# Batch 0's v on ScalarE's queue, chunks ahead of x, in the space of the later MLP weights

## The chip, the cores and the metric

One core of a Trainium2 chip runs the kernel. The metric is the device time of one execution in microseconds, the median of the timed runs; before the change this is 1745.4 us (three runs, 1744.48 to 1746.48). The core has TensorE (PE, products into PSUM), VectorE (DVE), ScalarE (ACT) and GpSimd (POOL), and SyncE (SP), which here only issues transfers. Transfers between HBM and SBUF run on 16 DMA engines; SyncE and ScalarE each have a queue from which they issue them. An engine works through its instructions in order; an instruction that waits holds up all behind it on that engine, transfers to be issued included.

## The reference

```python
def _attn_ref(x, v, pos_emb, w1, w2):            # x, v: [2, 12480, 128]
    h_mlp = np.maximum(pos_emb @ w1, 0.0) @ w2   # pos_emb [12480, 64]
    h_filt = h_mlp * np.exp(-0.01 * pos)[:, None]
    u = x * v
    Uf = np.fft.rfft(u, n=2 * S, axis=1); Hf = np.fft.rfft(h_filt, n=2 * S, axis=0)
    y = np.fft.irfft(Uf * Hf[None], n=2 * S, axis=1)[:, :S]
    return x * y
def _moe_ref(x, w_in, w_out):                    # 24960 tokens, 128 -> 2048 -> 128
    h = x @ w_in
    return np.maximum(0.01 * h, h) @ w_out
```

The output is the second function of the first: a long convolution of u = x * v with a filter from a small MLP over the positions, times x, then an MLP with 2048 hidden units. The weights `w_in` and `w_out` arrive as float64.

## The kernel before, in words

The convolution is a transform in two steps over token numbers n = 128 a + b (a up to 98, b up to 128), with spectra kept in HBM between the steps. For batch 0 the kernel has three stages: the first transforms along a (products with the constant `cf`, tiles `ft` and `f1`), the second along b, with the filter's product and the way back, and the third, the long one, transforms back and runs the MLP. Batch 1's convolution is a generator (`conv1`) whose pieces are taken in between. The instruction order is written out by hand (`manual_schedule`): every engine and every queue runs what the program text gives it, in that order.

The change lies in the first stage (from line 181, to about 166 us in the trace, its last store to 173). It has 16 chunks (`NC0 = HB // MC`) of 4 token columns for both halves p, each tile on 98 partitions:

- `load_pos(q)` fetches the positions of four chunks, `load_a(c)` fetches `ft`, x and v of a chunk (and `f1` for the first two). `load_tokens` issues three transfers for one tensor: 96 partitions, one partition, and the short last row (lines 68 and 70). In `load_a` all are on SyncE's queue; `ft` has 5 buffers, x and v 3 each.
- `prep(c)` multiplies x by v into `uh` (L212, on GpSimd, for chunk 0 on VectorE), computes `f1` from `ft` for chunks past the second (L221, L235, L236), and applies the small MLP to the positions (transposes L229, copy L232 on ScalarE, product L240, L243).
- For each of a chunk's four columns TensorE writes a PSUM tile `a` of three buffers (L315), and `add_sub` evacuates it: ScalarE copies one half to `a1s` (L99), VectorE forms sum and difference into the chunk's result `o` (L101, L103). `o` has two buffers.
- The result goes to HBM (`scr1`) in two transfers (L288). The store of chunk c-1 is kept in `late` and issued at the top of chunk c, behind `load_a(c + 3)`. So SyncE's order at the top of a chunk is: loads for three chunks on, positions if due, the store of the chunk before.
- `prep(c + 2)` is run in three steps between the columns of chunk c.
- At chunk 2 SyncE issues six small constant loads (`mb`, `mi`, `mi2`, L268 to L272), at chunk 7 `w22`, and at chunk 13 the first loads of batch 1 (`fetch_a(0)`). In the last chunk, one-row copies (`direct`, L308) and an early load (`early`, L303) bring `bin0`, the first tile of the second stage; the last store follows the last copies. The second stage's loads `bin` (L514) and the raw weights (L526, L527) stand behind it on SyncE's queue.
- The MLP weights live in four tiles of 8 KB per partition (`w_in_h`, `w_in_l`, `w_out_h`, `w_out_l`), taken from the pool `const` at the start (lines 52 to 55) and written only in the second stage (`weights`, L541 to L556).

## Time and profile before

| what | value |
|---|---|
| timed runs, median (lowest to highest) | 1745.4 us (1744.48 to 1746.48) |
| profiled execution, span from first to last instruction | 1742.2 us |
| busy share of the span: PE, DVE, ACT, POOL | 96%, 61%, 56%, 33% |
| transfers on SyncE's queue, on ScalarE's | 223.71 MB, 25.69 MB |
| mean rate of all transfers | 144 GB/s |

The profiled execution's own time is known by its span, 1742.2 us; the timed median has 3.2 us more, which lie around the first and last instruction or between two executions. The shares are means over the whole span, in which the third stage has most of the time; the first stage has 10% of it and other limits. A row of a view is read with its columns: in a table by stretch, the busy time of each engine in it, TensorE's granted clock as a share of full speed, the share of their time in which the 16 DMA engines were busy, and the rate at which they moved bytes.

### The profile page before, as it was taken

Reading aid. Unit: us, or ns where it says so; the run is one execution under the profiler, and the core shown is the slowest. Engines: PE = TensorE matmul, PEld = TensorE weight load, DVE = VectorE, ACT = ScalarE, POOL = GpSimd, SP = SyncE. Lnnn points to the kernel's source line nnn. Section 1 sums busy time; section 2 is a strip of 40 time slices with the busy share of each in tenths; the row PEclk is TensorE's granted clock in tenths of the full one; section 3 lists DMA queues with packets and bytes.
Section 4 is the critical chain, followed back from the end, with each engine's and each line's share of the span. In section 5 each row is a group of like instructions: output and inputs, shape, how many; then the busy total and the mean of one; then the engine's idle time right before and its main releaser. Section 6 shows DMA issues by size and latency. Waiting matters only on the chain.

```text
span 1742.2 us, 26075 instructions
## 1 busy us (share of the span) xinstructions
PE 1679.3 (96%) x9159; PEld 1383.3 (79%) x9159; DVE 1060.0 (61%) x1687; ACT 973.7 (56%) x1875; POOL 579.3 (33%) x474
## 2 busy tenths in 40 slices
PE   6788899899999999999999999999999999999998
PEld 6677555598888888888888888888888888888888
DVE  4566688744544555565555554567666676667665
ACT  1222455344444466666666665666666666666666
POOL 3453122232232165565555662222112121212110
PEclk9889899989999999999999999999999999999999
DMA  9998999865666565656555642312112121212110
GB/s 231 253 274 250 310 337 325 276 177 164 188 178 177 145 168 147 173 160 162 155 155 144 184 130 71 88 53 66 57 52 73 42 66 52 64 44 73 52 31 19
DMA packets 147687, 251.07 MB, mean 144 GB/s; under 512 B 10835, under 2 KB 96930, under 8 KB 144484
## 3 DMA queue, kind: packets, MB, share of 16 engines
q1 hardware_dynamic: 127412, 223.71, 45.9%
q10 hardware_dynamic: 20144, 25.69, 4.2%
q8 instruction: 73, 1.20, 0.3%
q14 instruction: 58, 0.48, 0.1%
HBM read 165.86 MB, written 83.43 MB: 143 GB/s over the span
## 4 chain that ended last, share of the span: by engine, by line
PE 81%; DMA 10%; DVE 5%; issue 1%; SPq 1%; ACT 1%; POOL 1%; ACTq 0%; DVEq 0%; POOLq 0%
PE mh L735 10%; PE acc L768 10%; PE mh L737 10%; PE acc L767 10%; PE acc L769 10%; PE mh L736 10%; PE yp L719 7%; PE cv L132 4%; PE cv L353 3%; DMA xt<-in_x_dram 2%; DMA ft<-in_cf_dram 2%; PE op L791 2%; DMA scr<-o 1%; DMA hspec<-hs 1%; PE xp L711 1%
## 5 line engine op out<-in xcount | busy, mean ns | idle before, releaser
L742 DVE SCALAR_TENSOR_TENSOR rl<-mh,rh 128x512 fp32r<-128x512 f32 (+2 forms) x400 | 269.1, 677 | 304.3 <-ACT rh L741 299.5
L752 DVE TENSOR_TENSOR rl<-r,rh 128x512 fp32r<-128x512 f32 (+1 forms) x400 | 292.5, 744 | 148.2 <-ACT rh L751 141.3
L735 PE MATMUL mh<-zh,w_in_h 128*128 128x512 f32 (+3 forms) x800 | 328.4, 411 | 2.8 <-DVE rl L742 1.5
L741 ACT ACTIVATE rh<-mh 128x512 fp32r<-128x512 f32 (+2 forms) x400 | 235.3, 591 | 157.0 <-PE mh L737 148.1
L768 PE MATMUL acc<-rl,w_out_h 128*128 128x512 f32 (+3 forms) x800 | 310.9, 389 | 0.1
L737 PE MATMUL mh<-zh,w_in_l 128*128 128x512 f32 (+3 forms) x800 | 310.4, 388 | 0.0
L767 PE MATMUL acc<-rh,w_out_h 128*128 128x512 f32 (+3 forms) x800 | 310.3, 388 | 0.0
L769 PE MATMUL acc<-rh,w_out_l 128*128 128x512 f32 (+3 forms) x800 | 310.0, 387 | 0.0
L736 PE MATMUL mh<-zl,w_in_h 128*128 128x512 f32 (+3 forms) x800 | 309.6, 387 | 0.0
L747 ACT ACTIVATE r<-mh 128x512 f32<-128x512 f32 (+1 forms) x400 | 235.7, 590 | 129.0 <-PE mh L737 115.1
L728 POOL TENSOR_TENSOR zl<-zf,zh 128x390 fp32r<-128x390 f32 (+24 forms) x110 | 67.9, 631 | 660.8 <-ACT zh L727 514.3
L768 PEld LDWEIGHTS acc<-rl,w_out_h 128*128 128x128 f32 x800 | 150.4, 188 | 38.5 <-DVE rl L752 8.3
L737 PEld LDWEIGHTS mh<-zh,w_in_l 128*128 128x128 f32 x800 | 150.8, 188 | 31.9
L769 PEld LDWEIGHTS acc<-rh,w_out_l 128*128 128x128 f32 x800 | 150.4, 188 | 30.3
L767 PEld LDWEIGHTS acc<-rh,w_out_h 128*128 128x128 f32 x800 | 150.4, 188 | 30.2
L735 PEld LDWEIGHTS mh<-zh,w_in_h 128*128 128x128 f32 x800 | 151.2, 189 | 27.7 <-DVE rl L742 4.1
L736 PEld LDWEIGHTS mh<-zl,w_in_h 128*128 128x128 f32 x800 | 151.4, 189 | 23.5 <-DVE zl L728 0.3
L749 DVE CAST rh<-r 128x512 fp32r<-128x512 f32 (+1 forms) x200 | 115.6, 578 | 31.2 <-ACT r L747 28.4
L719 PEld LDWEIGHTS yp<-g,cp 98*128 98x128 f32 x1024 | 125.7, 194 | 5.5 <-issue 0.5
L751 ACT CAST rh<-r 128x512 fp32r<-128x512 f32 (+1 forms) x200 | 122.3, 612 | 6.3
L719 PE MATMUL yp<-g,cp 98*128 98x97 f32 (+1 forms) x1024 | 125.0, 276 | 0.2 <-issue 0.2
L727 ACT CAST zh<-zf 128x390 fp32r<-128x390 f32 (+24 forms) x111 | 37.7, 380 | 154.0 <-DVE zf L722 154.0
(133 smaller groups left out, 2328.1 us busy)
## 6 DMA issues: line engine op xcount, KB each, us to landing
cin<-scr SPq DMA_DIRECT2D x64, 392.0 KB
hd<-hspec SPq DMA_DIRECT2D x48, 512.0 KB
g<-in_cg_dram SPq DMA_DIRECT2D x65, 300.1 KB
scr<-o SPq DMA_DIRECT2D x32, 588.0 KB
bin<-scr SPq DMA_DIRECT2D x23, 768.0 KB
scr1b<-o SPq DMA_DIRECT2D x32, 392.0 KB
xm<-in_x_dram SPq DMA_DIRECT2D x65, 192.0 KB
hspec<-hs ACTq DMA_DIRECT2D x48, 256.0 KB
```

Of the source, the lines that this page charges most:

```text
L719: nc.tensor.matmul(yp[:, at:at + n], ci_t[:, r, m, p, :], g[:, r, p, m, :n], start=(r == 0), stop=(r == 1))
L735: nc.tensor.matmul(hp, w_in_h[:, fs], zh, start=True, stop=False)
L736: nc.tensor.matmul(hp, w_in_h[:, fs], zl, start=False, stop=False)
L737: nc.tensor.matmul(hp, w_in_l[:, fs], zh, start=False, stop=True)
L741: nc.scalar.activation(out=rh, in_=hp, func=AF.Relu)
L742: nc.vector.scalar_tensor_tensor(out=rl, in0=hp, scalar=0.0, in1=rh, op0=ALU.max, op1=ALU.subtract)
L747: nc.scalar.activation(out=r, in_=hp, func=AF.Lrelu, alpha=0.01)
L751: nc.scalar.copy(rh, r)
L752: nc.vector.tensor_tensor(out=rl, in0=r, in1=rh, op=ALU.subtract)
L767: nc.tensor.matmul(ap, w_out_h[:, f, :], rh, start=(f == 0 and at0[k] >= S), stop=False)
L768: nc.tensor.matmul(ap, w_out_h[:, f, :], rl, start=False, stop=False)
L769: nc.tensor.matmul(ap, w_out_l[:, f, :], rh, start=False, stop=(f == NF - 1))
```

## The change

v of batch 0 no longer comes with x in `load_a`. A new function `load_v(upto)` issues v's loads on ScalarE's queue, chunk by chunk, up to a given number of chunks. They go into halves of four tiles of a new pool `wp`; the four tiles of the MLP weights take the same space (`tag` w0 to w3) after the first stage. `load_v(1)` stands ahead of all other loads, `load_v(3)` behind `load_a(1)`, and at the top of chunk c stands `load_v(min(2 * c + 5, c + 8))`, ahead of `load_a(c + 3)`. x has four buffers in place of three, `o` three in place of two.

```diff
--- before.py
+++ after.py
@@ -49,10 +49,7 @@
 
     ident = const.tile([128, 128], F32, name="ident")
     mb = const.tile([128, 2, 2, 64], F32, name="mb")
-    w_in_h = const.tile([128, DFF], F32R, name="w_in_h")
-    w_in_l = const.tile([128, DFF], F32R, name="w_in_l")
-    w_out_h = const.tile([128, NF, D], F32R, name="w_out_h")
-    w_out_l = const.tile([128, NF, D], F32R, name="w_out_l")
+    wp = ctx.enter_context(tc.tile_pool(name="wp", bufs=1, reuse_waits="tile"))
     wc_h = const.tile([128, D], F32R, name="wc_h")
     wc_l = const.tile([128, D], F32R, name="wc_l")
     mb_h = const.tile([128, 2, 128], F32R, name="mb_h")
@@ -61,13 +58,13 @@
     mi_h = const.tile([128, 2, 128], F32R, name="mi_h")
     mi_l = const.tile([128, 2, 128], F32R, name="mi_l")
 
-    def load_tokens(t, src, m0, n):
+    def load_tokens(t, src, m0, n, q=nc.sync):
 
         full = src[: ROWS * NB, :].rearrange("(a p n) d -> a p n d", p=2, n=HB)
         for r in (slice(0, R0), slice(R0, ROWS)):
-            nc.sync.dma_start(out=t[r], in_=full[r, :, m0:m0 + n, :])
+            q.dma_start(out=t[r], in_=full[r, :, m0:m0 + n, :])
         last = src[ROWS * NB + m0:ROWS * NB + m0 + n, :]
-        nc.sync.dma_start(out=t[ROWS:], in_=last[None, None, :, :].to_broadcast([1, 2, n, last.shape[1]]))
+        q.dma_start(out=t[ROWS:], in_=last[None, None, :, :].to_broadcast([1, 2, n, last.shape[1]]))
 
     def from_float64(pool, dst, src, n):
 
@@ -185,7 +182,19 @@
             w1bd = sba.tile([128, 128], F32, name="w1bd", bufs=1)
             mi = s0.tile([128, 2, 128], F32, tag="mi", name="mi", bufs=1)
             PQ = 16
-            pos_t, f_t, xv_t, uh_t, f1_t = {}, {}, {}, {}, {}
+            pos_t, f_t, x_t, uh_t, f1_t = {}, {}, {}, {}, {}
+            vbuf = []
+            for w in range(4):
+                t = wp.tile([128, DFF], F32, tag=f"w{w}", name="vt")
+                for i in range(2):
+                    vbuf.append(t[:NA, i * 1024:i * 1024 + 1024].rearrange("a (p m d) -> a p m d", p=2, d=D))
+            v_t = []
+
+            def load_v(upto):
+                while len(v_t) < min(upto, HB // MC):
+                    t = vbuf[len(v_t) % len(vbuf)]
+                    load_tokens(t, v[0], len(v_t) * MC, MC, nc.scalar)
+                    v_t.append(t)
             rot = sba.tile([NA, 2, NA], F32, name="rot", bufs=1)
 
             def load_pos(q):
@@ -195,18 +204,16 @@
             def load_a(c):
                 ft = sba.tile([NA, MC, 2 * NA], F32, tag="ft", name="ft", bufs=5)
                 nc.sync.dma_start(out=ft, in_=cf[:, c * MC:(c + 1) * MC, 0])
-                xt = sba.tile([NA, 2, MC, D], F32, tag="xt", name="xt", bufs=3)
-                vt = sba.tile([NA, 2, MC, D], F32, tag="vt", name="vt", bufs=3)
+                xt = sba.tile([NA, 2, MC, D], F32, tag="xt", name="xt", bufs=4)
                 load_tokens(xt, x[0], c * MC, MC)
-                load_tokens(vt, v[0], c * MC, MC)
-                f_t[c], xv_t[c] = ft, (xt, vt)
+                f_t[c], x_t[c] = ft, xt
                 if c < 2:
                     f1_t[c] = sba.tile([NA, MC, 2 * NA], F32, tag="f1", name="f1", bufs=3)
                     nc.sync.dma_start(out=f1_t[c], in_=cf[:, c * MC:(c + 1) * MC, 1])
 
             def prep(c):
 
-                xt, vt = xv_t.pop(c)
+                xt, vt = x_t.pop(c), v_t[c]
                 uh = sba.tile([NA, 2, MC, C0], F32, tag="uh", name="uh", bufs=3)
                 uh_t[c] = uh
                 (nc.gpsimd if c else nc.vector).tensor_tensor(out=uh[:, :, :, FO:], in0=xt, in1=vt, op=ALU.mult)
@@ -246,6 +253,8 @@
 
             NC0 = HB // MC
             DIR, EARLY = 1, 1
+            AHEAD_V = 8
+            load_v(1)
             load_pos(0)
             nc.vector.memset(w1bd, 0.0)
             for i in range(2):
@@ -255,11 +264,13 @@
             nc.sync.dma_start(out=win, in_=cw)
             nc.sync.dma_start(out=rot, in_=cr)
             load_a(1)
+            load_v(3)
             run(prep(0))
             load_a(2)
             run(prep(1))
             late = []
             for c in range(NC0):
+                load_v(min(2 * c + 5, c + AHEAD_V))
                 if c + 3 < NC0:
                     load_a(c + 3)
                     if (c + 3) * MC % PQ == 0:
@@ -280,7 +291,7 @@
                 late = []
                 uh, ft, f1 = uh_t.pop(c), f_t.pop(c), f1_t.pop(c)
                 nxt = prep(c + 2) if c + 2 < NC0 else iter(())
-                o = sba.tile([NA, 2, MC, 2, C0], F32, tag="o", name="o")
+                o = sba.tile([NA, 2, MC, 2, C0], F32, tag="o", name="o", bufs=3)
 
                 def store(m0, n, o, c=c):
                     for ri in range(2):
@@ -327,6 +338,10 @@
                     late.append(lambda store=store, o=o: store(0, MC, o))
 
 
+        w_in_h = wp.tile([128, DFF], F32R, tag="w0", name="w_in_h")
+        w_in_l = wp.tile([128, DFF], F32R, tag="w1", name="w_in_l")
+        w_out_h = wp.tile([128, NF, D], F32R, tag="w2", name="w_out_h")
+        w_out_l = wp.tile([128, NF, D], F32R, tag="w3", name="w_out_l")
         sc = ctx.enter_context(tc.tile_pool(name="sc", bufs=2, reuse_waits="tile"))
         psc = {}
         N1 = HB // MC1
```

## Rows read from the trace of the kernel before

**Rows 1.** The page's slices: DMA busy share in tenths, 40 equal slices.

```profile
DMA  9998999865666565656555642312112121212110
```

**Rows 2.** Waits, first stage: who waited for whom, us, times, longest.

```profile
DVE o L101 <- DMA scr<-o: 42.0, 12, 7.1
...
SPq L288 <- DMA ft<-in_cf_dram: 9.7, 9, 2.6
```

**Rows 3.** Busy times by stretch: us, engines' busy us (count), PEclk, DMA share, GB/s.

```profile
8.00:12.00 4.00, 2.85 (x14) 2.43 (x13) 0.00 (x0) 0.97 (x2) 0.00 (x0) 1.00 0.72 172
12.00:44.00 32.00, 25.78 (x134) 24.16 (x135) 17.77 (x29) 6.07 (x13) 16.68 (x10) 0.89 0.99 253
44.00:52.00 8.00, 6.39 (x44) 6.05 (x42) 3.76 (x8) 2.31 (x5) 4.95 (x3) 1.00 0.61 166
...
83.50:91.40 7.90, 7.90 (x54) 7.88 (x53) 5.81 (x11) 2.68 (x6) 3.96 (x3) 0.93 0.99 297
...
108.70:120.50 11.80, 7.76 (x29) 6.48 (x30) 5.81 (x11) 1.93 (x4) 4.89 (x3) 0.63 0.92 245
...
144.60:150.30 5.70, 4.58 (x27) 3.81 (x25) 5.70 (x11) 1.44 (x3) 1.88 (x2) 1.00 0.89 267
```

**Rows 4.** Transfers issued from 0 to 170 us: queue, count, size of one.

```profile
scr<-o SPq DMA_DIRECT2D x32, 588.0 KB
xt<-in_x_dram SPq DMA_DIRECT2D x16, 384.0 KB
...
ft<-in_cf_dram SPq DMA_DIRECT2D x16, 300.1 KB
pos<-in_pos_emb_dram SPq DMA_DIRECT2D x4, 768.0 KB
```

**Rows 5.** The chain that ended last: start us, us, what.

```profile
0.73 6.33 DMA pos<-in_pos_emb_dram
```

**Rows 6.** SyncE's issues in order of time: start us, us, line, transfer.

```profile
7.08 0.59 SPq L70 DMA_DIRECT2D xt<-in_x_dram  x1
7.71 1.23 SPq L68 DMA_DIRECT2D vt<-in_v_dram  x2
...
45.02 2.45 SPq L272 DMA_DIRECT2D mi<-in_ci_dram  x4
```

**Rows 7.** TensorE in order of time within one chunk.

```profile
87.32 0.81 PE L315 MATMUL a<-uh,ft 98*98 98x192 f32 x4
...
87.97 0.81 PE L315 MATMUL a<-uh,f 97*98 97x192 f32 x4
...
88.63 0.50 PE L229 MATMUL pt<-ident,pos 98*128 98x98 f32 x4
...
90.27 1.04 PE L240 MATMUL hp<-w1bd,pts 128*98 128x128 f32 x8
```

**Rows 8.** ScalarE's queue in the second stage: two issues each.

```profile
173.03 1.22 ACTq L650 DMA_DIRECT2D hspec<-hs  x2
...
183.92 2.29 ACTq L650 DMA_DIRECT2D hspec<-hs  x2
```

**Rows 9.** Busy times by stretch around the second stage, columns as in rows 3.

```profile
176.00:180.00 4.00, 1.95 (x16) 1.60 (x16) 0.42 (x1) 0.00 (x0) 0.00 (x0) 0.59 1.01 357
154.00:160.00 6.00, 3.29 (x21) 2.97 (x19) 1.87 (x4) 0.96 (x2) 2.35 (x1) 0.97 0.92 336
180.00:260.00 80.00, 76.98 (x621) 44.24 (x622) 63.74 (x139) 38.87 (x78) 15.31 (x12) 0.96 0.99 325
```

**Rows 10.** VectorE and SyncE at the end of the first stage, by time.

```profile
159.13 0.56 DVE L101 TENSOR_TENSOR o<-a,a1s 98x384 f32<-98x384 f32 x1 [4.13 <-DMA scr<-o]
...
160.18 2.57 SPq L308 DMA_DIRECT2D bin<-o  x4
...
162.85 0.85 SPq L303 DMA_DIRECT2D bin<-scr  x2
...
166.30 0.96 SPq L288 DMA_DIRECT2D scr<-o  x2
```

## The prediction

> **What bounds the kernel now.** The change touches the first 173 of 1742 us, so I read the page's slices first: the DMA row stands at 9, 9, 9, 8 in the first four of forty slices of 43.6 us [rows 1]. Next the list of waits in the first stage: VectorE stands 42.0 us, twelve times, before its addition into `o` (L101), each time until an earlier store of `o` has landed [rows 2]. That looks as if a third `o` would bring up to 42 us. The third view, busy times by stretch, says why it doesn't: in the same stretches the 16 DMA engines are 0.92 to 0.99 busy [rows 3]. VectorE waits for a store because that store stands in a full line of transfers; take this wait away, and the next one is for the loads in the same line. One chunk moves two stores of 588 KB, x and v of 384 KB each and 300 KB of `ft` [rows 4], 2.30 MB; at the 297 GB/s of 83.5 to 91.4 us that takes 7.7 us, and this stretch, one chunk without positions, lasts 7.9 [rows 3]. The engines could go faster: VectorE is busy 5.81 us of those 7.9 [rows 3], and TensorE's pairs of products come 0.65 us apart when nothing holds them, so eight pairs with 0.50 and 1.04 us of the next chunk's preparation make 6.7 us [rows 7]. So transfers bound the stage, the engines lie 1 us per chunk behind them, and what counts is (a) the time in which the DMA engines stand idle, (b) the rate at which they move bytes, (c) how the last chunk reaches the second stage. The change takes no byte away.
>
> **The sum's base.** The span of the profiled execution is 1742.2 us, 3.2 us under the 1745.4 us median of the timed runs; I take differences within the span and put them on the median.
>
> **What the change moves.** Of nine transfers that SyncE issues per chunk, three (v) go to ScalarE's queue, into the two halves of four 8 KB tiles that later hold the MLP weights. There are eight halves, so a half comes round after eight chunks, when its product is long done: no wait there, and the weights are written only in the second stage. x gets a fourth buffer and `o` a third. The order of v against x changes: v of chunk 0 first of all, chunks 1 and 2 before `prep(0)`, then two chunks of v per chunk of work until it is some five ahead.
>
> **(1) Gaps that are there now.** Against the 0.99 of 12 to 44 us, the DMA engines miss 0.27 x 4.0 = 1.1 us at 8 to 12 us, and 0.38 x 8.0 = 3.0 us at 44 to 52 us, where SyncE issues six small constant loads one behind the other (four of them take 2.45 us of issue) [rows 3, 6]. Later they miss 0.07 x 11.8 = 0.8 at 108.7 us and 0.10 x 5.7 = 0.6 at 144.6 [rows 3]. That is 4.1 us early and 1.4 us late. Late, when all v is loaded, a chunk has six transfers in place of nine, so that more of the next can be under way: I take -1.4 us there (ends -1.4 and 0), and the early ones within (2).
>
> **(2) Gaps that are new.** The compiled program gives its transfers eight completion semaphores in turn, in program order over both queues, so an issue waits until the transfer eight places before it has landed, whoever issued it. The trace shows it: the ninth issue (x, L70) starts at 7.08 us, when the first (positions) has landed at 0.73 + 6.33 = 7.06 [rows 5, 6]; and SyncE's store issues stand 9.7 us, nine times, for loads of `ft` that a store has no use for [rows 2]. With the change this ties the queues together. ScalarE's v issues stand at the top of a chunk; behind them wait its copies `a1s` (L99), then VectorE's `o` and TensorE's PSUM buffers. The third v issue of a chunk waits for `ft` of the chunk before; at chunk 2 one waits for the positions, at chunk 3 one for the small constants. In turn SyncE's x issue of the first chunks waits until a v has landed that ScalarE can issue only when it gets there. An issue takes 0.6 us (two of v on SyncE 1.23 [rows 6]; on ScalarE's queue two take 1.22, or 2.29 where the second had to wait [rows 8]): 1.8 us per chunk of v, 3.7 in chunks 0 to 3, and meanwhile TensorE can run ahead into three PSUM buffers.
>
> I laid the first 67 us out issue by issue with the trace's own times. The positions' 0.79 MB at 253 GB/s take 3.1 of their 6.33 us [rows 3 to 5], so 3.2 us go by between an issue and its first byte and between last byte and landing. At the same rate an x or v takes 1.6 us and an `ft` 1.2, and a chunk's stores 3.6 at 336 GB/s [rows 9]. `ft` of chunk 0 then waits for v's landing (6.8 us), chunk 0's first copy comes at 27 us, and gaps of 1 to 3 us open each time both queues hang on a landing: about 8, 24, 32, 40, 52, 57 and 66 us, 10.6 us together. At the same unhindered rates the kernel before moves, until 67 us, seven x, v and `ft`, two `f1`, two positions, three and a half chunks of stores and 1.6 us of constants: 53.6 us of 64.7, 11.1 us of gaps. So the two come out even, by then five chunks of v are in, and a chunk and a half of stores is behind. I take +1.0 us, with the 4.1 us of (1) inside. Ends: -4 (the old gaps filled, none new) and +6.5 (10.6 against the 4.1 that rows 3 show).
>
> **(3) The rate.** With v on a second queue, loads and stores run side by side more often. No second queue works in the first stage; the nearest rows are from the second, where both do: 357 GB/s at 176 to 180 us and 325 at 180 to 260, against 336 for stores nearly alone on one queue [rows 9] and 253 where loads predominate [rows 3]. Sixteen v of 1.3 us (at 297 GB/s), each beside another transfer, are some 42 us with both queues in use. At 325/0.99 in place of 297/0.99 GB/s they shrink by 8.5%, 3.6 us: I take -3.6, since those are the nearest rows with two queues, though their tiles are of all 128 partitions. Ends: 0, and -6.1 if each v goes from 253 to 336 GB/s (16 x 0.38). I take no loss: in no row are two queues slower than one.
>
> The Trainium skill speaks against this term: "DMA: Bandwidth & Descriptors", section "Issuing engines are not separate DMA queues", says that transfers begun by several engines run on the same 16 DMA engines and interleave, so that a second issuer saves only issue time. By that the gain would be 3.6 us smaller.
>
> **(4) The tail.** VectorE's first `o` of the last chunk waits 4.13 us, until 159.13, for the store of two chunks before. SyncE then issues four one-row copies into `bin0` from 160.18, the early load of `bin0` at 162.85, four more copies, and the last store at 166.30 [rows 10]; the second stage's first full load waits for that store. With a third `o` the results are 4 us earlier, the first copies go while the two stores before are still moving, and the early load goes when these land. That saves at least the 0.3 us in which the later copies wait, at most this and the 2.57 us of the first copies: ends -0.3 and -2.9. I take -1.0, because the line of stores is full until about the first copies. All that follows moves along, since the second stage starts with transfers again (0.99 busy from 180 to 260 us [rows 9]).
>
> **(5) At nothing.** SyncE's saved issues (covered by the transfers under way; without that cover 1.8 us per chunk), the fourth x (x waits for no buffer now), and other places in SBUF.
>
> **Sum:** +1.0 - 1.4 - 3.6 - 1.0 = -5.0 us, 1745.4 - 5.0 = **1740.4 us**.
>
> **The rivals.**
> *A, one pool of engines, no rate gained:* (3) is 0, and +1.0 - 1.4 - 1.0 leaves 1744.0 us. For it: shares near 1 already [rows 3], so that only gaps can be won.
> The skill's rule above would end here too.
> *B, the queues chain each other (slower):* ScalarE's issues at the tops of chunks 0 to 3 come late, SyncE's loads hang on them, and the DMA engines run dry: +6.5 for (2), 0 for the late gaps and (3), -1.0 for the tail: 1750.9 us. For it: store issues that already stand for foreign loads [rows 2], the ninth issue [rows 5, 6], and a computing engine now in the same chain. Against it: the gaps are short, and the engines have 1 us of room per chunk. It decides when the DMA engines miss more than some 9 us between 12 and 68 us. That v doesn't get ahead as the change says belongs here: its third issue hangs on `ft` of one chunk before.
> *C, full overlap:* (3) at -6.1, (2) at -1: -9.5, 1735.9 us. Against it: TensorE bounds a chunk at 6.7 us.
>
> **How the numbers follow.** Forecast 0.40, A 0.27, B 0.21, C 0.12. A measurement of this kernel tells about 0.2% (3.5 us) from no change, so faster means under 1741.9: forecast and C, 0.52; same 0.27; slower 0.21. The range takes in the forecast, A, C with the long end of the tail, and the nearer half of B: 1733.5 to 1748.5. Forecast and C alone have 1733.5 to 1742.
>
> **What would show it.** (1): no stretch of 8 us with a share near 0.6 around 44 us. (2): idle in front of `a1s` at the tops of chunks 0 to 3, released by loads; the first `a1s` near 27 us. (3): over 297 GB/s in chunks 4 to 8. (4): no wait for a store before the last `o`, and the last store before 166 us. VectorE's 42 us of waits for stores should be near nothing. I am wrong if the last store goes out later although the rate rose (then the gaps of (2) are larger), or over 8 us earlier (then transfers did not bound as I say, and the `o` wait was a cause of its own).

## The result: slower, and where the time goes

The kernel with the change takes 1760.2 us (median of four runs, 1757.8 to 1768.0) where the kernel before takes 1745.3 beside it: a ratio of 1.0087 with a 95% interval of 1.0068 to 1.0107, 15 us more. The forecast was 1740.4, with a range up to 1748.5. The profiled span is 1756.0 us, 13.8 us over that of before; the result's line numbers differ a little (`a1s` L96, `o` L98 and L100, `load_tokens` L65 and L67, the stores L299, the positions' copies L239).

Nearly all of the loss lies in the first stage. SyncE issues its last store at 179.27 us; before, it was at 166.30 [rows 10]. That is 13.0 of the 13.8 us.

```profile
168.50 4.70 SPq L319 DMA_DIRECT2D bin<-o  x4
174.70 1.97 SPq L314 DMA_DIRECT2D bin<-scr  x2
...
179.27 0.96 SPq L299 DMA_DIRECT2D scr<-o  x2
```

The busy times by stretch, columns as in rows 3, first of before and then of after, tell where in the stage:

```profile
12.00:84.00 72.00, 54.84 (x297) 50.99 (x298) 40.10 (x73) 16.33 (x36) 36.43 (x21) 0.86 0.94 253
84.00:120.00 36.00, 29.54 (x172) 26.79 (x172) 22.77 (x44) 8.86 (x19) 19.77 (x12) 0.88 0.95 269
120.00:160.00 40.00, 34.78 (x214) 32.20 (x212) 28.12 (x54) 11.26 (x24) 18.10 (x11) 0.97 0.94 287
```

```profile
12.00:84.00 72.00, 47.98 (x241) 44.18 (x242) 31.46 (x54) 12.56 (x27) 27.51 (x16) 0.83 0.84 221
84.00:120.00 36.00, 31.74 (x199) 29.62 (x198) 28.73 (x52) 11.41 (x26) 22.04 (x12) 0.95 0.94 265
120.00:160.00 40.00, 32.42 (x204) 31.36 (x203) 31.32 (x52) 10.69 (x23) 26.22 (x15) 0.87 0.87 259
```

From 12 to 84 us, 72 x (253 - 221) = 2.3 MB fewer are moved, 9.1 us at the old rate; from 84 to 120 it is 0.5 us and from 120 to 160 (28 x 40 = 1.1 MB at 287) 3.9 us. The sum, 13.5, is about the delay of the last store. The times of the stores say it from the other side: the first goes out 8.6 us later than before (42.36 for 33.77), the fourth 15.1 us (78.95 for 63.86), the tenth 11.5 (132.75 for 121.21). So 15 us are lost in the first chunks, 3.6 come back while v is ahead, and part of that goes again at the end, when no v is left to load.

Over the whole stage, from the start to the end of its last store (first before, then after):

```profile
0.00:167.30 167.30, 129.78 (x729) 119.81 (x730) 94.22 (x177) 40.26 (x85) 75.00 (x50) 0.89 0.91 255
0.00:180.30 180.30, 126.91 (x736) 118.77 (x736) 104.30 (x180) 40.20 (x86) 78.83 (x50) 0.89 0.85 237
```

Both move some 42.7 MB (time x rate). The DMA engines are busy for about 152 and 153 us of these stretches (time x share) and idle for 15 and 27. The loss is idle time of the transfers, not a lower rate.

What the waits show (who waited for whom, us, times, longest):

```profile
DVE o L98 <- ACT a1s L96: 43.5, 20, 9.0
ACT a1s L96 <- DMA vt<-in_v_dram: 39.0, 8, 9.6
...
ACT L239 <- DMA vt<-in_v_dram: 11.6, 1, 11.6
```

and of SyncE's queue:

```profile
SPq L65 <- DMA vt<-in_v_dram: 19.8, 5, 8.4
...
SPq L299 <- DMA vt<-in_v_dram: 6.4, 3, 3.4
```

VectorE's 42.0 us of waits for stores [rows 2] are gone, as forecast. In their place VectorE waits 43.5 us for ScalarE's copy (9.7 before). ScalarE's own rows for v come to 54.4 us. They hold the issuing too, because this view doesn't count it as busy time: summed over the timeline, the 48 issues take about 33 us, and for about 21 us ScalarE stands because an issue may not start yet. SyncE stands 32.5 us for v (0.5 before). By stretch one sees computing and transfers take turns:

```profile
32.00:40.00 8.00, 3.71 (x17) 3.29 (x15) 4.84 (x9) 1.13 (x3) 7.92 (x5) 0.69 1.04 259
40.00:44.00 4.00, 4.00 (x23) 3.94 (x22) 3.23 (x5) 0.69 (x2) 1.37 (x2) 0.77 0.40 104
44.00:48.00 4.00, 3.20 (x22) 2.85 (x20) 2.09 (x5) 0.48 (x1) 3.67 (x2) 1.00 0.92 249
48.00:52.00 4.00, 0.00 (x0) 0.00 (x0) 0.00 (x0) 0.00 (x0) 0.41 (x1) 1.00 0.96 246
52.00:60.00 8.00, 5.91 (x25) 5.62 (x26) 4.08 (x8) 1.73 (x4) 0.88 (x1) 0.57 0.48 138
60.00:64.00 4.00, 3.09 (x21) 2.74 (x19) 1.82 (x4) 0.48 (x1) 3.78 (x2) 1.00 0.92 247
64.00:68.00 4.00, 0.00 (x0) 0.00 (x0) 0.00 (x0) 0.00 (x0) 0.29 (x1) 0.71 0.98 253
```

Where the DMA share (last column but one) is 0.40 or 0.48, TensorE (first) is busy; where it is 0.96 or 0.98, TensorE does nothing at all.

TensorE's clock lengthens such a phase of computing. TensorE had stood since 47.2 us and comes back at 54.1 at a granted clock of 0.50 (1.2 of 2.4 GHz). ScalarE then waits 4.34 us for its products; at the same place of a later chunk, at full clock, it waits 2.07. The first three rows are of after, the last is of before, which has a stretch at 0.50 too, but with the DMA engines at 0.92:

```profile
53.00:58.00 5.00, 3.91 (x15) 3.72 (x16) 3.35 (x6) 1.25 (x3) 0.88 (x1) 0.50 0.49 147
58.76 0.48 ACT L96 COPY a1s<-a 98x384 f32<-98x384 f32 x1 [4.34 <-PE a L326]
82.81 0.48 ACT L96 COPY a1s<-a 98x384 f32<-98x384 f32 x1 [2.07 <-PE a L326]
56.00:60.00 4.00, 3.93 (x13) 3.59 (x14) 4.00 (x8) 0.96 (x2) 0.93 (x2) 0.50 0.92 274
```

How much of the 15 us this makes, no run isolates.

Issue by issue, SyncE first (start us, us that the issues took, line, transfer):

```profile
43.28 1.09 SPq L206 DMA_DIRECT2D ft<-in_cf_dram  x1
52.86 1.27 SPq L65 DMA_DIRECT2D xt<-in_x_dram  x2
...
60.64 9.46 SPq L65 DMA_DIRECT2D xt<-in_x_dram  x2
70.15 0.60 SPq L67 DMA_DIRECT2D xt<-in_x_dram  x1
```

and ScalarE's queue with its copies:

```profile
44.36 2.50 ACTq L65 DMA_DIRECT2D vt<-in_v_dram  x2
...
52.48 0.57 ACTq L67 DMA_DIRECT2D vt<-in_v_dram  x1
53.17 0.48 ACT L96 COPY a1s<-a 98x384 f32<-98x384 f32 x1 [8.36 <-DMA vt<-in_v_dram]
...
60.30 2.51 ACTq L65 DMA_DIRECT2D vt<-in_v_dram  x2
...
69.58 0.58 ACTq L67 DMA_DIRECT2D vt<-in_v_dram  x1
70.28 0.48 ACT L96 COPY a1s<-a 98x384 f32<-98x384 f32 x1 [9.58 <-DMA vt<-in_v_dram]
```

ScalarE comes to the top of a chunk at 44.36 and issues the first v; its own sixth issue (52.48) and SyncE's next x (52.86) both stand until that v has landed. The same at 60.30: SyncE's second x transfer starts some 9 us later, and so does ScalarE's last issue. In the compiled program, and in the trace's records, these two issues wait on the completion semaphores (the marks that a transfer has landed) of the two v transfers that begin at 60.30.

### The profile page after: what moved, and what is told of

Read it like the earlier page. It is cut to its first block, busy times and chain, and to the rows that moved or that the text cites. A ratio compares the mean times of both kernels' runs of the same rounds, so it can differ in the third digit from the quotient of the medians.

```text
span 1756.0 us, 26073 instructions
## 1 busy us (share of the span) xinstructions
PE 1674.9 (95%) x9159; PEld 1380.1 (79%) x9159; DVE 1068.2 (61%) x1687; ACT 971.7 (55%) x1875; POOL 582.5 (33%) x474
## 4 chain that ended last, share of the span: by engine, by line
PE 81%; DMA 7%; DVE 7%; issue 2%; SPq 1%; ACT 1%; POOL 1%; ACTq 0%; POOLq 0%; DVEq 0%
PE mh L750 10%; PE acc L783 10%; PE mh L752 10%; PE acc L782 10%; PE mh L751 10%; PE acc L784 10%; PE yp L734 6%; PE cv L129 4%; PE cv L368 3%; DMA vt<-in_v_dram 2%; PE a L326 2%; PE op L806 2%; DVE ta L123 1%; PE xp L726 1%; DVE tb L123 1%
```

## The experiments

Times are medians beside runs of the kernel before on the same chip; each ratio is against those, with its 95% interval. The last four columns come from the profiled execution: DMA share and rate from 12 to 84 us, all of SyncE's waits for v and ScalarE's idle time for v up to 180 us (its own issuing included, where it lies in such a gap), and the start of the last store. A profiled execution need not be the median one: e3_act_with_x's was 7.3 us over its median, e16_wait's 4.4, e9_pool_with_x's 4.0 and e5_sync_with_x's 2.7, e24_both's 3.8 and e15_pool_consts's 3.4 under theirs.

| kernel | v issued by | time us | ratio, interval | DMA, GB/s | SyncE for v | ScalarE for v | last store |
|---|---|---|---|---|---|---|---|
| before | SyncE, with x | 1745.3 | | 0.94, 253 | 0.5 | 0 | 166.3 |
| the change | ScalarE, lead | 1760.2 | 1.0087 (1.0068 to 1.0107) | 0.84, 221 | 32.5 | 54.4 | 179.3 |
| e2_sync | SyncE, lead | 1745.7 | 1.0008 (0.9998 to 1.0019) | 0.91, 249 | 6.4 | 0 | 166.6 |
| e3_act_with_x | ScalarE, with x | 1758.8 | 1.0093 (1.0069 to 1.0118) | 0.84, 225 | 43.1 | 31.8 | 190.1 |
| e5_sync_with_x | SyncE, with x | 1743.3 | 0.9997 (0.9986 to 1.0009) | 0.91, 248 | 0 | 0 | 167.7 |
| e4_pool | GpSimd, lead | 1737.3 | 0.9960 (0.9944 to 0.9976) | 0.97, 265 | 0 | 0 | 160.2 |
| e9_pool_with_x | GpSimd, with x | 1737.2 | 0.9953 (0.9936 to 0.9971) | 0.95, 268 | 0 | 0 | 159.2 |
| e12_pool_fewer | GpSimd, lead | 1737.5 | 0.9955 (0.9937 to 0.9972) | 0.98, 272 | 0 | 0 | 160.0 |
| e7_busy | SyncE, with x | 1744.7 | 0.9993 (0.9983 to 1.0004) | 0.93, 250 | 0.2 | 0 | 165.5 |
| e16_wait | SyncE, with x | 1743.8 | 0.9996 (0.9981 to 1.0012) | 0.93, 238 | 1.6 | 37.7 | 166.9 |
| e18_tied | SyncE, with x | 1743.7 | 0.9993 (0.9980 to 1.0007) | 0.92, 251 | 0.4 | 0 | 168.5 |
| e24_both | SyncE, with x | 1747.1 | 1.0018 (1.0003 to 1.0034) | 0.88, 232 | 0.4 | 40.1 | 169.2 |
| e13_x_pool | ScalarE, with x | 1742.1 | 0.9974 (0.9962 to 0.9987) | 0.90, 243 | 10.7 | 48.4 | 166.1 |
| e14_x_pool_lead | ScalarE, lead | 1759.3 | 1.0092 (1.0071 to 1.0112) | 0.78, 202 | 9.4 | 41.5 | 180.1 |
| e10_loads_pool | ScalarE, lead | 1760.6 | 1.0081 (1.0058 to 1.0104) | 0.80, 217 | 16.8 | 44.0 | 180.4 |
| e25_act_pos_pool | ScalarE, with x | 1759.6 | 1.0090 (1.0059 to 1.0121) | 0.87, 240 | 46.7 | 20.3 | 180.7 |
| e26_sync_pos_pool | SyncE, with x | 1742.4 | 0.9982 (0.9968 to 0.9996) | 0.92, 248 | 0 | 0 | 166.4 |
| e17_before_pool | GpSimd, with x | 1739.6 | 0.9962 (0.9945 to 0.9979) | 0.97, 271 | 0 | 0 | 160.1 |
| e21_before_pool_consts | GpSimd, with x | 1737.7 | 0.9964 (0.9951 to 0.9976) | 0.97, 272 | 0 | 0 | 159.6 |
| e15_pool_consts | GpSimd, with x | 1734.4 | 0.9932 (0.9911 to 0.9953) | 0.98, 272 | 0 | 0 | 156.6 |

### Which part of the change loses: queue, lead or buffers

Four kernels undo one or two parts. The queue alone (lead and buffers stay):

```diff
-                    load_tokens(t, v[0], len(v_t) * MC, MC, nc.scalar)
+                    load_tokens(t, v[0], len(v_t) * MC, MC)              # e2_sync
+                    load_tokens(t, v[0], len(v_t) * MC, MC, nc.gpsimd)   # e4_pool
```

The lead alone (e3_act_with_x; e5_sync_with_x takes the queue back too):

```diff
                 load_tokens(xt, x[0], c * MC, MC)
+                load_v(c + 1)
...
-            load_v(1)
             load_pos(0)
...
-            load_v(3)
...
-                load_v(min(2 * c + 5, c + AHEAD_V))
```

> Only the queue of batch 0's v is undone: same early order of v, same buffers, but SyncE issues it. Theory of the chained queues (the loss is ScalarE's copies standing behind v's issues, and SyncE's loads behind v's landing): ScalarE never waits for a load before a1s, and most of the 15 us come back, 1742 to 1750 us; chunk 3's first copy near 62 us in place of 70.3. Rival of early loading (v takes transfer time from what the first chunks need, whoever issues it): 1756 to 1762 us. Rival of space (third o, fourth x, other places in SBUF): 1756 to 1762 us.

> Only the lead of v is undone: v comes with x, three chunks on as before, still on ScalarE's queue and in the space of the weights. Chained queues: ScalarE still issues three transfers at the top of each chunk and stands behind others' landings, now in all 16 chunks but with three and not six issues in the first ones: 1750 to 1765 us, and a1s still waits for loads. Early loading: 1742 to 1748 us. Space: 1756 to 1762 us.

> Queue and lead of v both undone (SyncE, with x, as before); what is left of the change is v in the weights' space, a third o and a fourth x. Chained queues and early loading: 1741 to 1746 us, VectorE's waits for stores before o (42.0 us before) under 10 us, and the tail 0.3 to 2.9 us shorter, as I forecast for the third o. Space: 1756 to 1762 us.

> v in the same early order, but issued by GpSimd, whose transfers take completion semaphores of their own, so that neither ScalarE nor SyncE waits for v's places. Chained queues: ScalarE free of load waits, SyncE's loads no longer wait for v: 1738 to 1750 us, less what GpSimd pays for its own issues. Early loading: 1756 to 1762 us. Space: 1756 to 1762 us.

On SyncE's queue the lead costs nothing and brings nothing (1.0008), and the buffers and the weights' space do neither (0.9997). On ScalarE's queue v costs 15 us without any lead (1.0093). So the loss needs ScalarE's queue and does not need the lead. e4_pool was the surprise: the same early order on GpSimd's queue is faster than the kernel before, by 0.4%. The compiled program gives the transfers of SyncE and ScalarE eight completion semaphores in common, and those of GpSimd eight others; the traces' records name the same ones, issue by issue.

In e3_act_with_x the loss is to be seen at the positions' loads (an issue of SyncE, one of ScalarE, then two stretches):

```profile
80.01 9.28 SPq L65 DMA_DIRECT2D pos<-in_pos_emb_dram  x2
```

```profile
79.45 1.32 ACTq L65 DMA_DIRECT2D vt<-in_v_dram  x2
```

```profile
84.00:88.00 4.00, 0.00 (x0) 0.00 (x0) 3.46 (x4) 0.00 (x0) 3.77 (x2) 0.56 0.69 159
88.00:92.00 4.00, 0.53 (x4) 0.56 (x5) 0.00 (x0) 0.00 (x0) 1.91 (x2) 0.50 0.26 75
```

The second transfer of the positions starts 9 us after the first, because its place among the eight is the one of the v that ScalarE issued at 79.45; TensorE has nothing to do, and at last neither have the DMA engines (0.26). In the compiled program that v stands ahead of `ft` and x of its chunk (places 86 and 87 for v, 88 for `ft`, 94 for the positions' second transfer), and the trace's records have the semaphores in this order, but v was issued after them (`ft` at 76.17 us). So a place is held by a transfer that has not yet been issued, and what comes eight places later waits for ScalarE to arrive and then for the whole transfer.

### What about ScalarE: its time, its waits, or what hangs on it?

e7_busy holds ScalarE without transfers, e16_wait makes it wait for landings without issuing, e18_tied makes SyncE's v wait for ScalarE, e24_both does both. All stand on e5_sync_with_x, with `pad` a small scratch tile:

```diff
             for c in range(NC0):
+                for _ in range(8 if c < 4 else 4):                         # e7_busy, [128, 512]
+                    nc.scalar.copy(pad, w1bd[:, :1].to_broadcast([128, 512]))
+                if c + 2 < NC0:                                            # e16_wait
+                    nc.scalar.copy(pad[:NA, :2], v_t[c + 2][:, :, 0, 0])
```

```diff
                     t = vbuf[len(v_t) % len(vbuf)]
+                    if len(v_t) >= 3:                                      # e24_both only
+                        nc.scalar.copy(pad2[:NA], v_t[-1][:, :, 0, 0])
+                    nc.scalar.copy(t[:, :, 0, 0], pad[:NA])                # e18_tied, e24_both
                     load_tokens(t, v[0], len(v_t) * MC, MC)
```

> v on SyncE's queue, loaded together with x (as in e5_sync_with_x), and ScalarE copies a scratch tile of 512 columns four times at the top of every chunk, eight times in chunks 0 to 3. One such copy should take about 0.59 us, so that ScalarE is held for 2.3 us per chunk and 4.7 us in the first four: a quarter more than the change's issues of v hold it where none of them waits (two of 0.61 and one of 0.57 us). If ScalarE's issues cost what their waits cost (my theory now), time in which ScalarE is merely occupied costs little: 1742 to 1748 us. If ScalarE simply has no room at the top of a chunk (rival), this kernel is as slow as the change: 1755 or more.

> v on SyncE's queue, together with x (as e5_sync_with_x, 1743.3 us), and ScalarE issues nothing, but at the top of each chunk it copies two numbers per partition out of the v that lands for the chunk after next. So ScalarE waits for about the landing that an issue of v would wait for, eight transfers back, and does no issue. If waiting in front of a1s is the cause (my theory), the loss is here without any issue of ScalarE: 1750 to 1762 us, ScalarE idle 20 to 40 us for v, and the last store several us later than the 167.65 of e5_sync_with_x. If it is ScalarE's queue or its issues, this stays at 1742 to 1748.

> v on SyncE's queue, together with x (as e5_sync_with_x, 1743.3 us), but ScalarE writes two numbers per partition into v's buffer at the top of a chunk, before SyncE may load v into it. ScalarE waits for no landing and issues nothing; SyncE's loads can't run further ahead than ScalarE has come. If it is enough that loads hang on ScalarE's progress: 1750 to 1762 us, with DMA shares under 0.6 where TensorE is busy. If it needs both directions (ScalarE waiting for landings too), it stays at 1742 to 1748.

> e16_wait and e18_tied together: at the top of a chunk ScalarE first reads two numbers per partition of the v loaded one chunk before, then writes two into the buffer of the next v, which SyncE may only load after that. So ScalarE waits for a landing and a load waits for ScalarE, as in the change, but every transfer is issued by SyncE. If computing and transfers then take turns (my theory now), the loss is here with no issue on ScalarE's queue: 1752 to 1766 us, DMA share at most 0.88 from 12 to 84 us (0.94 before, 0.84 with the change). If the loss needs transfers issued by ScalarE, 1742 to 1748.

e7_busy: the eight copies hold ScalarE for 5.16 us at the top of a chunk, where six unhindered issues of v take 3.6, and there is no loss (0.9993). e16_wait was a miss for my theory of that time: ScalarE waits longer for v, 37.7 us, than the 21 or so of the change, and nothing is lost.

```profile
ACT pad L273 <- DMA vt<-in_v_dram: 37.7, 8, 14.6
```

The transfers go on meanwhile, because SyncE issues them and doesn't stand. e18_tied costs nothing either (0.9993). Both directions together cost 3.8 us against e5_sync_with_x (1747.1 for 1743.3; the intervals of the two ratios touch), with the DMA share at 0.88 from 12 to 84 us as expected, but that is a quarter of the loss, below the 1752 that I had expected. The ties hardly closed, though: up to 180 us SyncE stood 0.8 us for ScalarE in e18_tied and 4.8 in e24_both, against the 32.5 us for v with the change. So these two kernels do not show what a SyncE that really stands would cost. In e24_both all transfers have one issuer, so places and issues are in one order, and no place is held by a transfer that is still to be issued. It leaves out two issuers in one round of places, and with them SyncE's long waits.

### Taking transfers out of the common round

e13_x_pool is e3_act_with_x with x issued by GpSimd, e14_x_pool_lead the change with the same, e10_loads_pool the change with x and `ft` by GpSimd; e25_act_pos_pool is e3_act_with_x with the positions of chunks 4 to 15 by GpSimd, and e26_sync_pos_pool its counterpart with v on SyncE's queue.

```diff
-                load_tokens(xt, x[0], c * MC, MC)
+                load_tokens(xt, x[0], c * MC, MC, nc.gpsimd)               # e13, e14, e10
-                nc.sync.dma_start(out=ft, in_=cf[:, c * MC:(c + 1) * MC, 0])
+                nc.gpsimd.dma_start(out=ft, in_=cf[:, c * MC:(c + 1) * MC, 0])   # e10
-                load_tokens(pos_t[q], pos_emb, q * PQ, PQ)
+                load_tokens(pos_t[q], pos_emb, q * PQ, PQ, nc.gpsimd if q else nc.sync)  # e25, e26
```

> The change with v still on ScalarE's queue and at its places, 48 issues of it, but x and ft issued by GpSimd, so that ScalarE's issues share the eight semaphores with the stores, positions and constants only. If the chain of loads on one set of semaphores is the cause, ScalarE's idle time in front of a1s for v falls from 39 us to under 10, and the time to 1736 to 1746 us (GpSimd has four issues of about 0.6 us per chunk more beside 5.3 us of work, which may cost some us of that). If ScalarE's queue is slow in itself, or its 48 issues are, the loss stays: 1755 or more.

> v on ScalarE's queue together with x (as e3_act_with_x, 1758.8 us), but x issued by GpSimd. It is e9_pool_with_x (1737.2) with the queues of x and v exchanged. Per chunk six transfers in place of nine share the eight semaphores, so an issue of ScalarE waits for one that is 1.3 chunks old in place of 0.9. If waits are the cause, ScalarE's idle time for v falls from the 32 us of e3_act_with_x to 5 to 20, and the time lies between: 1740 to 1752 us. If any issue on ScalarE's queue costs what it costs whatever it shares, 1756 or more.

> e13_x_pool (x issued by GpSimd, v by ScalarE, 1742.1 us) with the lead of the change: two v per chunk in chunks 0 to 3. It stands between e13_x_pool and e10_loads_pool (1760.6), which has the lead and ft on GpSimd's queue too. If it is the lead that makes ScalarE wait for its own six transfers per chunk, 1750 to 1762 us. If it is ft on GpSimd's queue, 1740 to 1746.

> e3_act_with_x (v on ScalarE's queue, together with x, 1758.8 us) with the positions of chunks 4 to 15 issued by GpSimd. In e3_act_with_x TensorE stands 27.4 us for positions, three times (13.5 us before), because SyncE can't issue their second transfer until a v has landed that ScalarE issued late. If that is where its loss lies, most of the 15 us come back: 1740 to 1749 us, TensorE's waits for positions at 14 us or less. If the chained v hurts wherever it meets a load (stores and x in the place of positions), 1754 or more.

> The same with v on SyncE's queue (e5_sync_with_x, 1743.3 us, with the positions of chunks 4 to 15 issued by GpSimd): what moving the positions is worth where no transfer is issued by ScalarE. 1738 to 1744 us, since their own semaphores let them go early as v's do in e17_before_pool, but they are three transfers in four chunks, not twelve. With e25_act_pos_pool it gives the price of ScalarE's queue without the positions in its chain.

e13_x_pool has v on ScalarE's queue and loses nothing against the kernel before: 1742.1 us, with SyncE's waits for v down from 43.1 to 10.7 us. It also has x on GpSimd's queue, though, and that queue gains by itself: against e9_pool_with_x, its counterpart with the queues of x and v exchanged, it is some 4 us slower by the ratios (0.9974 for 0.9953, with intervals that overlap). So most of the loss goes, but perhaps not all. The time came out as expected and the reason not, since ScalarE's idle time did not fall (48.4 us). This and e16_wait suggest the same: ScalarE may wait, as long as SyncE does not stand for it. e25_act_pos_pool missed: TensorE's waits for positions fell from 27.4 to 9.7 us, but SyncE's for v did not fall (46.7 us), they now sit in front of stores, x and the small constants, and the loss is the same 15 us (17 against e26_sync_pos_pool, its counterpart without ScalarE's queue). So the place that I had picked from the rows was only where the wait happened to fall. TensorE's row and SyncE's two largest in e25_act_pos_pool:

```profile
PE pt L237 <- DMA pos<-in_pos_emb_dram: 9.7, 1, 9.7
```

```profile
SPq L296 <- DMA vt<-in_v_dram: 23.7, 6, 5.7
SPq L65 <- DMA vt<-in_v_dram: 10.6, 2, 7.0
```

e10_loads_pool was a miss too, and e14_x_pool_lead tells why: with the lead the loss is back (1759.3 against 1742.1), though SyncE hardly waits for v (9.4 us). Here it is ScalarE itself, which at the top of each of the first chunks has six issues:

```profile
53.22 1.25 ACTq L65 DMA_DIRECT2D vt<-in_v_dram  x2
54.51 0.58 ACTq L67 DMA_DIRECT2D vt<-in_v_dram  x1
56.11 2.63 ACTq L65 DMA_DIRECT2D vt<-in_v_dram  x2
58.78 1.75 ACTq L67 DMA_DIRECT2D vt<-in_v_dram  x1
60.65 0.48 ACT L96 COPY a1s<-a 98x384 f32<-98x384 f32 x1 [7.47 <-issue]
```

It is held 5.4, 7.5 and 6.5 us in front of three chunks, and 15 issues of v (five chunks) stand ahead of its very first copy of `a1s`, which comes at 32.45 us. The first store goes out at 41.12 us (33.95 in e13_x_pool), the fourth at 82.54 (63.50). The same 15 issues stand ahead of the first copy in the change. That ScalarE's own issues make this loss is read from these rows; no run isolates it, and in e7_busy 5.16 us of other work at the same places cost nothing.

### GpSimd's queue: what it gains, and a faster version

e9_pool_with_x is e5_sync_with_x with v on GpSimd's queue, e12_pool_fewer is e4_pool with two buffers for `o` and three for x, e17_before_pool is the kernel before with v's three transfers issued by GpSimd and nothing else, and e15_pool_consts and e21_before_pool_consts put five of the six small constants of chunk 2 on GpSimd's queue too, in e9_pool_with_x and in e17_before_pool:

```diff
-                load_tokens(vt, v[0], c * MC, MC)
+                load_tokens(vt, v[0], c * MC, MC, nc.gpsimd)               # e17, e21
-                    nc.sync.dma_start(out=mi, in_=ci)
+                    nc.gpsimd.dma_start(out=mi, in_=ci)                    # e15, e21; the four mi2 likewise
```

> v on GpSimd's queue as in e4_pool, but without the lead: v of a chunk is issued together with its x, three chunks ahead. If what e4_pool wins (1737.3) comes from transfers that no longer share eight completion semaphores with SyncE's, this is as fast: 1735 to 1740. If it comes from the lead, which GpSimd's queue alone can build up, this falls back to the kernel before: 1743 to 1747.

> e4_pool (v on GpSimd's queue, with the lead) with two buffers for o and three for x, as the kernel before has them. If buffers bound nothing as long as the transfers do, it is within 2 us of e4_pool, 1735 to 1740, and VectorE's waits for stores before o are back at 20 to 45 us. If the freed queue needs them, 1742 or more.

> The kernel before with one thing changed: v's three transfers per chunk are issued by GpSimd. No lead, no third o, no fourth x, no space of the weights. If all of what e4_pool and e9_pool_with_x win comes from the queue with semaphores of its own, 1735 to 1740 us. If it needs the buffers or the space too, 1742 to 1746.

> e9_pool_with_x (v on GpSimd's queue, together with x) with five of the six small constant loads of chunk 2 on GpSimd's queue too. The gap at 44 to 52 us (share 0.73 in e9_pool_with_x, so 2.1 us missing against 0.99) closes if SyncE's issues of these constants open it: 1734 to 1737 us. If the gap has another cause, or GpSimd's 3 us of issues take the place of it, no change: 1737 to 1740.

> The kernel before with two things changed: v's transfers and five of the six small constants of chunk 2 are issued by GpSimd. If e15_pool_consts (1734.4 us, with a third o, a fourth x and v in the weights' space) owes nothing to buffers and space, 1732 to 1738. If it does, 1739 to 1744, like e17_before_pool.

The lead is not what GpSimd's queue needs (e9_pool_with_x is as fast as e4_pool), nor are the buffers: with two `o`, VectorE's waits for stores are back at 22.7 us, and the time stays.

```profile
DVE o L98 <- DMA scr<-o: 22.7, 11, 5.2
```

One argument on the kernel before (e17_before_pool) gives 0.9962. From 84 to 120 us the rate is 291 GB/s for 269 before, at about the same share:

```profile
12.00:84.00 72.00, 59.96 (x324) 55.21 (x323) 47.22 (x77) 17.33 (x38) 50.30 (x44) 0.91 0.97 271
84.00:120.00 36.00, 30.77 (x187) 29.23 (x186) 29.66 (x48) 9.79 (x21) 28.05 (x27) 0.91 0.97 291
```

But e2_sync, with all transfers on SyncE's queue, moves 285 GB/s at a share of 0.95 in that stretch. Over the whole stage, to the end of the last store, e2_sync (first) and e17_before_pool have:

```profile
0.00:167.60 167.60, 127.50 (x736) 120.51 (x736) 105.96 (x180) 40.87 (x86) 82.48 (x50) 0.88 0.88 254
0.00:161.10 161.10, 127.49 (x736) 118.87 (x736) 108.66 (x178) 40.22 (x85) 103.32 (x98) 0.93 0.92 264
```

For the same bytes the DMA engines are busy about 147 us in e2_sync and 148 in e17_before_pool (152 before), and idle about 20 and 13 (15 before). One queue reaches the same rate; what e2_sync lacks is filled gaps.

The constants on GpSimd's queue bring e15_pool_consts to 1734.4 us, 0.7% under the kernel before (0.9911 to 0.9953), the fastest of all. From 44 to 52 us its share is 0.90 where e9_pool_with_x has 0.73 (these two rows, e9_pool_with_x first):

```profile
44.00:52.00 8.00, 7.12 (x49) 6.81 (x48) 8.00 (x12) 2.74 (x6) 6.77 (x7) 1.00 0.73 196
```

```profile
44.00:52.00 8.00, 4.48 (x22) 3.95 (x21) 8.00 (x12) 1.49 (x4) 7.00 (x7) 0.83 0.90 285
```

In the kernel before's own setting (e21_before_pool_consts, 0.9964) the constants bring nothing beyond e17_before_pool by the intervals, so that the 2.8 us between e9_pool_with_x and e15_pool_consts are not settled.

## Why the prediction was wrong, step by step

**What bounds the kernel: right.** Transfers bound the stage, and the 42 us of waits for stores were no cause of their own: with a third `o` they go and the time stays (e5_sync_with_x), and with two on GpSimd's queue they come back and the time stays (e12_pool_fewer).

**(1) The gaps that are there now: half right.** Around 44 us the share is no longer 0.61 but 0.92 and 0.96; yet the constants now go out at 54.8 us, and the gap is there (0.48 from 52 to 60 us). The 1.4 us of late gaps were not won: from 120 to 160 us the share fell from 0.94 to 0.87. By then all of v is loaded (its last issue is at 110.41 us), and from 140 to 160 us TensorE is busy for all of the 20 us at a share of 0.79: the engines are the bound there.

**(2) The new gaps: this is the step that failed, in its size.** I took +1.0 us with +6.5 as the far end; the rates from 12 to 84 us give about 9 us, and the fourth store 15. By 67 us, where my layout had both kernels even, the change has moved 67 x (231 - 206) = 1.7 MB less (before, then after):

```profile
0.00:67.00 67.00, 46.57 (x248) 43.33 (x249) 31.17 (x55) 13.91 (x28) 28.16 (x22) 0.90 0.89 231
0.00:67.00 67.00, 36.20 (x176) 32.75 (x176) 21.62 (x37) 8.98 (x18) 22.37 (x18) 0.89 0.81 206
```

The mechanism was named, and the first `a1s` came near where I had put it (25.0 for 27). Three things in the working were wrong. I gave out the eight semaphores in the order of the program text; the compiled program mixes the two queues, and gives v a place ahead of loads that SyncE issues long before ScalarE gets there. I counted ScalarE's issues by their own time and let the copies run ahead into PSUM buffers; e7_busy bears this part out, but the issues wait, so that in the change the copies of a chunk come only after a landing, and VectorE and TensorE with them. And I compared gaps up to 67 us as if all bytes were alike, after finding that "a chunk and a half of stores is behind": v loaded ahead was set against stores that were late. Of the 15 us at the fourth store, only 3.6 came back by the tenth.

**(3) The rate: nothing gained.** From 12 to 84 us the change moves 221 / 0.84 = 263 GB/s per share for 253 / 0.94 = 269 before: nothing gained on ScalarE's queue, where I had estimated 8.5% for the v transfers. On GpSimd's queue the stage's transfers take about 148 us for 152, but e2_sync has that on SyncE's queue alone; why its transfers are shorter is open. The Trainium skill's rule ("DMA: Bandwidth & Descriptors", section "Issuing engines are not separate DMA queues"), by which a second issuer saves only issue time, agrees with these rows as to the rate. That a second issuer can lose 15 us stands on no row of before.

**(4) The tail: not told.** I took -1.0 us for the third `o`. In e5_sync_with_x, which has it, VectorE's waits for stores fall to 0.2 us, and the last store starts at 167.65 us against 166.30, but in an execution 2.7 us over its median. Its interval, -2.4 to +1.6 us, neither shows nor excludes 1 us.

**(5) At nothing: right for the buffers and the space.** The fourth x and the weights' space moved no time by the intervals (e5_sync_with_x, e12_pool_fewer). For SyncE's saved issues no run decides: GpSimd's kernels save them too, and gain 0.4 to 0.5% from causes that are not separated.

**The sum.** By the bytes, (2) came to 9.1 us in place of 1.0, the later stretches to 4.4 in place of -1.4, and (3) and (4) together to about nothing in place of -4.6: 13.5 of the 13.8 us in the span.

**The rivals.** Rival B, queues that chain each other, is what happened, at nearly three times its price (+14.9 us for +5.5). Its point of decision, some 9 us missing between 12 and 68 us, was not quite reached: at a share of 0.85 there, 7.8 us are missing against 0.99. Against it I had held that the engines have 1 us of room per chunk; the chain costs a whole landing each time it closes, 6.2 to 9.6 us of ScalarE's time, issues included, in front of `a1s` at the tops of chunks 0 to 3. Rivals A and C priced the rate, which never came to bear.

**What is shown and what stays open.** Shown: the loss is idle time of the DMA engines, and it needs v's issues on ScalarE's queue (e2, e3, e4). Neither ScalarE's time, up to 5.16 us per chunk (e7), nor its waiting (e16) costs anything by itself. With the lead off, most of the loss goes when x leaves the common round (e13), and none when the positions do (e25); with the lead on, it comes back (e14, e10). Argued from rows and not isolated: that in e14 and e10 it comes through ScalarE's own issues, and that elsewhere it comes from places held by a v not yet issued, for which SyncE stands. e18 and e24 don't decide this, since SyncE hardly stood in them, and no kernel here has two issuers in one round of places with the places in the order of the issues. How the change's 15 us divide between these causes and TensorE's lower clock is open as well: e3 and e14 lose that much by one cause each, and the change, which has both, no more.

## What to carry to other kernels

A queue on another engine is not a free line: where its transfers share completion semaphores with the busy queue, each queue can come to stand until the other has arrived and its transfer has landed, and an engine that computes arrives late. Before moving loads, look in the compiled program at which issue each issue waits for, and at what that engine does first. And a wait that looks expensive is only worth its length if the transfers stop with it: ScalarE's 38 us of waits cost nothing while SyncE went on issuing, and VectorE's 42 us went without a gain.

## What the runs showed of the hardware

GpSimd's issues, which I had not considered, were the best place for v. An issue takes 0.62 us of GpSimd's time (32 of them 19.7 us in e4_pool; the short last rows 0.50), on an engine that is busy, these issues included, for 105.7 of the first 176 us there, and still the kernel gained 0.4%. With v on it the last store starts at 159.2 to 160.2 us, against 166.3 before and 166.6 with the lead on SyncE's queue (156.6 with the constants on GpSimd's too). The rate of a single stretch does not tell the queues apart: from 84 to 120 us GpSimd's kernels moved 285 to 303 GB/s, and those with SyncE alone 259 to 285.
